# Moving the transposes inside a forward DFT from TensorE to DMA transposes

## The chip, the cores and the metric

The kernel runs on one core of a Trainium2 chip. Its time is the device time of one execution in microseconds (us); of several executions the median is taken. The core has five engines with a queue each, which run in order: PE (TensorE, matrix products), DVE (VectorE), ACT (ScalarE), POOL (GpSimd) and SP (SyncE, which here issues nearly all DMAs). The DMAs of all queues are carried by 16 DMA engines.

## The reference

The program computes one layer and all its gradients (a forward pass, then its vector-Jacobian product with `grad_out`), for one sequence of L = 2048 steps and D = 512 channels in bf16:

```
xn  = layernorm(A_u)
K   = Re( sum_n C * exp(dt*A)^l * dt*B )           # a kernel of 2048 taps per channel, N = 128 states
s   = causal_conv(xn, K)  + xn * Dskip             # the reference does it with FFTs of length 4096
g   = silu( silu(xn @ w1) @ w2 )                   # F = 1792
out = A_u + s * g
```

It returns `out` and the gradients of `A_u`, the six state matrices, `log_dt`, `Dskip`, `w1` and `w2`.

## The kernel before, in words

Time is cut as 128 partitions times T = 16 steps, channels into NB = 4 blocks of 128. The stages, in the order of the time axis of the profile (us from the start of the span):

- 0 to about 50: layer norm, tables, the parameters of the state matrices.
- 50 to about 245: `gen_ffn_fwd` (L574, both products of the FFN) beside the first part of `gen_ssm_fwd` (L509), which makes the convolution kernels `K_b` and parks the tables `XT` and `YT` of each eighth of a block in DRAM.
- 247 to about 624: `gen_conv` (L623) for blocks 0 to 3. Beside blocks 0 to 2 runs the rest of `gen_ssm_fwd`, beside block 3 the first part of `gen_ssm_bwd` (L762).
- 624 to about 710: `gen_dw2` (L661), the gradient of `w2`; 710 to about 850: `gen_dh` (L687), the gradient of the hidden layer and of `w1`; then `gen_dx` (L730) and `gen_ssm_final` (L809). `gen_ssm_bwd` runs beside these.

**One block of the convolution.** `gen_conv` makes the DFTs of the normalised input (`UX`), of the kernel `K_b` (`KX`) and, later, of the gradient (`DX`), with three products in frequency (`cplx_mul`, L135, on DVE) and three inverse DFTs (`dft_inv`, L111): the forward result `S_b`, the gradient to the input `DXC` and that to the kernel `dKs`, each written to DRAM by a DMA (L642, L645, L652, L657). The write of `dKs` (L657, to `dk_d`) is the last act of a block.

**One forward DFT** (`dft_fwd`, L78) of 2048 points for 128 channels has three steps:

1. L87: 32 small products with the table `TF` into PSUM; eight evictions by ACT (L74, 128x512 each) write them to `A` (`dftA` in the profile), real and imaginary part (c = 0, 1), reordered as 16 groups g of (t, e).
2. L95: for each of 2 x 16 blocks of 128x128 a TensorE transpose against the identity into a PSUM tile `pt_b` that holds eight; four ACT copies (L74, 128x1024 bf16) bring them to `B` (`dftB`).
3. L102 and L103: 16 products with the constant matrices C2, S2, nS2, which mix both parts of `B`; eight evictions to `X` (by ACT, or by DVE at L105 for the real part of `KX`).

`A` and `B` have one buffer each, and `dft_inv` uses the buffer of `A` as well. So a DFT cannot refill `A` before its transposes have been read, and there is no more than one DFT of a kind in flight. Four blocks of three DFTs make 12 calls.

**What sets the order.** The stages are Python generators that `interleave` (L38) merges by weights; `BoundedGen` limits how many steps of a neighbour go beside a block. That gives each instruction its place in the program. The tile framework then lays out each engine's queue itself: it takes instructions by their place in the program, but passes over one whose operands it doesn't expect yet, by its own estimate of durations. This order is fixed when the program is built; on the chip each engine follows it and waits where an operand is late. One sees it in the trace: the transposes `DOT` at L677 belong to `gen_dw2`, after block 3 in the program, and three of them are issued between 544 and 556, inside block 3.

**DMA transposes** are in the kernel already, all issued by SP with DRAM as their source: the parameters (L417), `A_ft` (L670, 128 rows of 2048, 512 KB), `DOT` (L677, 2048 rows of 128, 512 KB each), `W2T` (L673) and `W1T` (L735).

Of the kernel before, what the change touches and what calls it, by code (L numbers as in the profile page):

```python
# [11 lines left out]
BF16 = mybir.dt.bfloat16  # L12
I32 = mybir.dt.int32
AX = mybir.AxisListType
P = 128
# [62 lines left out]
def dft_fwd(k, U, X, ev, addc=None):  # L78
    nc, big, psum, psumT = k.nc, k.cbig, k.psum, k.psumT
    G = 16  # L80
    TF = k.consts["TF"]
    A = big.tile([P, 2, G, 16, 8], BF16, name="dftA", tag="dftA")
    for t0 in range(0, 16, 4):
        for c in range(2):
            ps = psum.tile([P, 4, P], F32, name="ps_s1", tag="ps")
            for j in range(4):
                nc.tensor.matmul(out=ps[:, j, :], lhsT=TF[:, t0 + j, c, :], rhs=U[:, t0 + j, :], start=True, stop=True)  # L87
            ev(A[:, c, :, t0:t0 + 4, :], ps[:].rearrange("p t (g e) -> p g t e", e=8))
        yield
    B = big.tile([P, 2, G, P], BF16, name="dftB", tag="dftB")  # L90
    for g0 in range(0, G, 8):
        for c in range(2):
            pt = psumT.tile([P, 8, P], BF16, name="pt_b", tag="pt")
            for gi in range(8):
                nc.tensor.transpose(out=pt[:, gi, :], in_=A[:, c, g0 + gi, :, :].rearrange("p t e -> p (t e)"), identity=k.ident[:])  # L95
            ev(B[:, c, g0:g0 + 8, :], pt[:])
        yield
    C2, S2, nS2 = k.consts["C2"], k.consts["S2"], k.consts["nS2"]
    for g0 in range(0, G, 4):
        for c, (m0, m1) in enumerate(((C2, S2), (nS2, C2))):  # L100
            ps = psum.tile([P, 4, P], F32, name="ps_s2", tag="ps")
            nc.tensor.matmul(out=ps[:], lhsT=m0[:], rhs=B[:, 0, g0:g0 + 4, :], start=True, stop=False)  # L102
            nc.tensor.matmul(out=ps[:], lhsT=m1[:], rhs=B[:, 1, g0:g0 + 4, :], start=False, stop=True)  # L103
            if c == 0 and addc is not None:
                nc.vector.tensor_tensor(out=X[:, c, g0:g0 + 4, :], in0=ps[:], in1=addc[:, g0:g0 + 4].unsqueeze(2).to_broadcast([P, 4, P]), op=ALU.add)  # L105
            else:
                ev(X[:, c, g0:g0 + 4, :], ps[:])
        yield
# [514 lines left out]
def gen_conv(k, b):  # L623
# [8 lines left out]
    mk = lambda nm, tag: cb.tile([P, 2, 16, P], BF16, name=nm, tag=tag)  # L632
    UX = mk("UX", "UX"); DX = mk("DX", "DX"); KX = mk("KX", "KX")
    yield from dft_fwd(k, k.xn[:, :, blk], UX, k.ev)
    yield from dft_fwd(k, k.K_b[b][:], KX, k.ev, addc=k.dskx[:, 16 * b:16 * b + 16])
    YX = mk("YX", "PX")
    cplx_mul(k, YX, KX[:], UX[:])
# [7 lines left out]
    nc.sync.dma_start(k.o0_v[:, :, blk], g_b)  # L645
    yield
    yield from dft_fwd(k, ds_b, DX, k.ev)
    cplx_mul(k, KX, KX[:], DX[:], conj_a=True)
    yield
# [264 lines left out]
```

## Time and profile before

| | |
|---|---|
| time, median of 3 (lowest to highest) | 1028.93 us (1026.76 to 1033.08) |
| profiled execution | 1033.08 us, its span 1031.3 us |
| PE, weight loads, DVE, ACT busy | 731.1, 444.3, 735.1, 619.0 us |
| queue q1 (SP's DMAs) | 147.23 MB, 54.6% of the 16 engines' span |

The profiled execution is the slowest of the three; sums below are made against it. In the page's rows of instruction groups a line reads: source line, engine, operation, written tile <- read tile, shape, count, then busy time, mean duration in ns, and idle time of the engine just before, with what ended it. L74 is the helper `Evac`, so the tile tells which eviction it is.

By convolution block, cut where `dk_d` is written, the busy time of each engine is:

| block | window | length | PE | DVE | ACT | DMA share |
|---|---|---|---|---|---|---|
| 0 | 247 to 354 | 107 | 75.6 | 103.5 | 93.6 | 0.51 |
| 1 | 354 to 468 | 114 | 81.6 | 103.5 | 99.1 | 0.39 |
| 2 | 468 to 542 | 74 | 58.0 | 42.4 | 63.4 | 0.55 |
| 3 | 542 to 624 | 82 | 62.8 | 48.2 | 68.6 | 0.76 |

### The profile page before, as it was taken

How to read it: one execution, taken by the hardware profiler on the slowest of the kernel's cores; microseconds unless marked ns; L12 is line 12 of the kernel's file. 1: busy time of each engine (PE TensorE's matmuls, PEld its weight loads, DVE VectorE, ACT ScalarE, POOL GpSimd, SP SyncE). 2: the span in 40 equal slices, each digit the busy share in tenths (PEclk: the TensorE clock that was granted, in tenths of full speed). 3: DMA queues.
4: the chain of work that ended last, by engine and by line, in shares of the span. 5: the costliest groups of instructions: out<-in, count | busy, mean ns of one | idle time of the engine just before them, and what ended most of it. 6: DMA issues, size and time to landing. Idle time of an engine off the chain costs nothing. (4 is left out here: it accounts for less than half of the span.)

```text
span 1031.3 us, 16058 instructions
## 1 busy us (share of the span) xinstructions
PE 731.1 (71%) x6215; PEld 444.3 (43%) x6281; DVE 735.1 (71%) x1196; ACT 619.0 (60%) x1062; POOL 20.7 (2%) x85
## 2 busy tenths in 40 slices
PE   0277878997866677678777774787889897699500
PEld 0144545455555465556555442333444443244200
DVE  6998888999999979996552780223756665478942
ACT  0698878898998798969879771111332434344110
POOL 2100000000000000001100000000000000000000
PEclk9878989998989888879989998899999998699855
DMA  5064655667327312642589499998544647676410
GB/s 117 10 214 168 170 194 170 210 227 183 110 63 188 81 62 62 168 89 103 106 167 208 112 203 241 203 235 201 163 153 140 177 123 199 184 219 187 114 25 22
DMA packets 240383, 154.03 MB, mean 149 GB/s; under 512 B 175729, under 2 KB 209906, under 8 KB 240306
## 3 DMA queue, kind: packets, MB, share of 16 engines
q1 hardware_dynamic: 238962, 147.23, 54.6%
q0 software_dynamic: 768, 3.67, 1.1%
q10 hardware_dynamic: 576, 2.10, 0.6%
q8 instruction: 49, 0.80, 0.3%
q14 instruction: 28, 0.23, 0.1%
HBM read 74.84 MB, written 62.13 MB: 133 GB/s over the span
## 5 line engine op out<-in xcount | busy, mean ns | idle before, releaser
L74 ACT CAST Vb<-psV 128x512 bf16<-128x512 f32 x128 | 67.5, 624 | 76.0 <-PE psV L785 75.4
L506 DVE TENSOR_TENSOR X<-T_511 128x1024 bf16<-128x1024 bf16 x128 | 84.4, 704 | 14.7 <-PE ps_k L556 14.7
L532 PE MATMUL pf_t<-ident_bfloat_78,X 128*128 128x128 bf16 x1024 | 76.6, 230 | 22.9 <-DVE X L506 8.6
L532 PEld LDWEIGHTS <-X 128*128 128x128 bf16 x1024 | 67.9, 104 | 33.3 <-issue 17.2
L74 ACT CAST XTf<-pf_t 128x512 bf16<-128x512 f32 x128 | 67.0, 636 | 3.6 <-PE pf_t L532 3.6
L604 PE MATMUL ps_o<-W_410,aT 128*128 128x512 bf16 x215 | 54.0, 398 | 3.5 <-ACT th_2187 L608 1.2
L590 PE MATMUL ps_h<-XNT,W_408 128*128 128x512 bf16 x210 | 53.1, 389 | 2.6 <-ACT th L594 1.5
L705 PE MATMUL ps_da<-DOT,W2T 128*128 128x512 bf16 x224 | 53.1, 379 | 0.0
L746 PE MATMUL ps_dx<-W1T,dhT 128*128 128x512 bf16 x216 | 52.3, 388 | 0.7 <-issue 0.5
L785 PE MATMUL psV<-XT,Gbd 128*128 128x256 bf16 x256 | 45.5, 301 | 9.8 <-DMA XT<-xt_d 7.7
L60 DVE TENSOR_TENSOR T_511<-PC 128x896 bf16<-128x896 f32 (+1 forms) x40 | 51.7, 1348 | 0.4 <-ACT PC L452 0.4
L74 ACT COPY DH<-pt_dh 128x1024 bf16<-128x1024 bf16 x28 | 27.9, 1033 | 37.0 <-PE pt_dh L712 36.9
L680 PEld LDWEIGHTS <-A_ft 128*128 128x128 bf16 x224 | 23.0, 106 | 59.6 <-DMA A_ft<-at_d 30.1
L74 ACT COPY dftB<-pt_b 128x1024 bf16<-128x1024 bf16 x48 | 46.0, 1052 | 2.0 <-PE pt_b L95 1.6
L785 PEld LDWEIGHTS <-Gbd 128*128 128x128 bf16 x256 | 34.1, 177 | 27.9 <-issue 23.1
L706 DVE SCALAR_TENSOR_TENSOR dhT<-th_ft,ps_da 128x512 bf16<-128x512 bf16 x56 | 35.6, 682 | 8.4 <-PE ps_da L705 8.2
L698 DVE TENSOR_SCALAR th_ft<-th_ft 128x2048 bf16<-128x2048 bf16 x14 | 9.7, 693 | 43.9 <-DMA th_ft<-th_d 43.9
L556 PEld LDWEIGHTS <-X 128*128 128x128 bf16 x1024 | 35.9, 100 | 6.1 <-issue 1.5
L87 PEld LDWEIGHTS <-TF 128*128 128x128 bf16 x384 | 28.1, 106 | 23.1 <-issue 21.7
L556 PE MATMUL ps_k<-YY,X 128*128 128x64 bf16 x1024 | 37.6, 195 | 0.4
L594 ACT ACTIVATE th<-ps_h 128x512 bf16<-128x512 f32 x56 | 37.8, 675 | 0.0
L593 ACT ACTIVATE aT<-ps_h 128x512 bf16<-128x512 f32 x56 | 37.4, 669 | 0.5 <-PE pf_t L532 0.3
(1581 smaller groups left out, 1881.0 us busy)
## 6 DMA issues: line engine op xcount, KB each, us to landing
xt_d<-XTf SPq DMA_DIRECT2D x32, 512.0 KB, 2.8
XT<-xt_d SPq DMA_DIRECT2D x32, 512.0 KB, 5.1
YT<-yt_d SPq DMA_DIRECT2D x64, 256.0 KB, 4.6
yt_d<-YTf SPq DMA_DIRECT2D x32, 256.0 KB, 2.4
th_d<-th SPq DMA_DIRECT2D x28, 256.0 KB, 2.2
at_d<-aT SPq DMA_DIRECT2D x4, 1792.0 KB, 6.9
a_ft<-at_d SPq DMA_DIRECT2D x14, 512.0 KB, 3.7
th_ft<-th_d SPq DMA_DIRECT2D x14, 512.0 KB, 4.2
```

The costliest lines, as they stand in the source:

```text
L60: nc.vector.tensor_tensor(out=out, in0=a, in1=b, op=ALU.mult)
L74: self.nc.scalar.copy(out=out, in_=in_)
L506: nc.vector.tensor_tensor(out=out.rearrange("p (r h l u) -> p r h l u", h=nh, l=4, u=2), in0=h, in1=l, op=ALU.mult)
L532: nc.tensor.matmul(out=pf[:, qi, m // 2, :], lhsT=X[:, m, q + qi], rhs=k.ident[:], start=(m % 2 == 0), stop=(m % 2 == 1))
L556: nc.tensor.matmul(out=ps[:, q].rearrange("p e j -> p (e j)"), lhsT=X[:, m, q], rhs=YY[:, m // 2, q // 2, 1, 64 * (q % 2):64 * (q % 2) + 6 ...
L590: nc.tensor.matmul(out=ps[:], lhsT=W1[:, dk, ft * P:(ft + 1) * P], rhs=XNT[:, dk, 4 * tcn:4 * tcn + 4, :], start=(dk == 0), stop=(dk == DK ...
L593: nc.scalar.activation(out=aT[:, ft, :], in_=pf, func=ACT.Silu)
L594: nc.scalar.activation(out=th[:, s], in_=pf, func=ACT.Tanh, scale=0.5)
L604: nc.tensor.matmul(out=pso[:], lhsT=aT[:, ft, tt * P:(tt + 1) * P], rhs=W2[:, ft, :], start=(ft == 0), stop=(ft == FT - 1))
L705: nc.tensor.matmul(out=ps[:], lhsT=k.W2T[:, dk, rows], rhs=k.DOT[:, dk, ls], start=(dk == 0), stop=(dk == DK - 1))
L746: nc.tensor.matmul(out=ps[:], lhsT=k.dhT[:, ft, t * P:(t + 1) * P], rhs=W1T[:, ft, :], start=(ft == 0), stop=(ft == FT - 1))
L785: nc.tensor.matmul(out=psV[:, qi].rearrange("p a b -> p (a b)"), lhsT=Gbd[:, :, :, :, 32 * (q_ // 2 % 2) + 4 * c + 2 * (q_ % 2) + q_ // 4] ...
```

## The change

Step 2 of the forward DFT is replaced. In place of 32 TensorE transposes and four ACT copies, two DMA transposes issued by SP, one for the real and one for the imaginary part, go straight from `A` to `B`, both in SBUF. Each moves 128 rows of 2048 elements (512 KB) and leaves `B` in the same layout as before. The two yields of the step become one, so a DFT has one step less in the merging of the generators.

```diff
@@ dft_fwd
     B = big.tile([P, 2, G, P], BF16, name="dftB", tag="dftB")
-    for g0 in range(0, G, 8):
-        for c in range(2):
-            pt = psumT.tile([P, 8, P], BF16, name="pt_b", tag="pt")
-            for gi in range(8):
-                nc.tensor.transpose(out=pt[:, gi, :], in_=A[:, c, g0 + gi, :, :].rearrange("p t e -> p (t e)"), identity=k.ident[:])
-            ev(B[:, c, g0:g0 + 8, :], pt[:])
-        yield
+    for c in range(2):
+        nc.sync.dma_start_transpose(out=B[:, c], in_=A[:, c].rearrange("p g t e -> p (g t e)"))
+    yield
     C2, S2, nS2 = k.consts["C2"], k.consts["S2"], k.consts["nS2"]
```

## The prediction, made before the result

> **What bounds the kernel now.** I read the page first (twelve DFTs: 48 copies of `dftB` on ACT), then the busy time of each engine by convolution block, then the timeline of ACT and PE in one DFT, then the waits, and last the rows of the DMA transposes that the kernel has already.
>
> From the page, the two groups that go (the second only in its TensorE line):
>
> ```profile
> L74 ACT COPY dftB<-pt_b 128x1024 bf16<-128x1024 bf16 x48 | 46.0, 1052 | 2.0 <-PE pt_b L95 1.6
> ```
>
> ACT spends 46.0 us on these copies; TensorE's transposes at L95 fill 29.9 us of its time between 247 and 624.
>
> The busy times by block (length; PE, PEld, DVE, ACT, POOL; clock, DMA share, GB/s):
>
> ```profile
> 247.00:354.00 107.00, 75.60 (x957) 60.86 (x961) 103.54 (x148) 93.64 (x167) 0.00 (x0) 0.89 0.51 117
> 354.00:468.00 114.00, 81.64 (x1005) 65.76 (x1009) 103.45 (x153) 99.13 (x173) 0.00 (x0) 0.85 0.39 98
> 468.00:542.00 74.00, 57.98 (x681) 43.23 (x682) 42.41 (x60) 63.44 (x117) 7.01 (x2) 0.93 0.55 127
> 542.00:624.00 82.00, 62.81 (x554) 40.19 (x554) 48.22 (x63) 68.64 (x127) 0.00 (x0) 0.98 0.76 178
> ```
>
> Two regimes. In blocks 0 and 1 DVE is busy 97% and 91% of the time: the work of `gen_ssm_fwd` bounds them. In blocks 2 and 3 DVE is at 57% and 59%, and ACT at 86% and 84%: here the chain of one block, step after step through single buffers, sets the length, and most of its steps end in an ACT eviction. The blocks follow each other without overlap: SP issues the last write of a block (L657) at 354.5, 468.3, 542.6 and 623.6, and the first eviction of the next block's `dftA` comes within some 1 us of it. `A_ft`, the first transfer of the next stage, waits for the end of block 3: it is issued at 625.5. So the chain's length passes on to what follows.
>
> One DFT on ACT (start, duration), block 1, `KX`:
>
> ```profile
> 383.20 0.79 ACT L74 CAST dftA<-ps_s_4843 128x512 bf16<-128x512 f32 x1
> 383.68 0.85 ACT L74 CAST KF<-ps_k 64x256 bf16<-64x256 f32 x2
> 384.55 3.76 ACT L74 COPY dftB<-pt_b 128x1024 bf16<-128x1024 bf16 x4
> ```
>
> From the end of the last `dftA` eviction (384.0) to a complete `dftB` (388.3) it takes 4.3 us. Read in the same way, the twelve steps take 4.2 to 6.1 us, the longer ones with an eviction of another tile in between; the mean of the eleven that I read is 4.9 us. That is the time the change replaces.
>
> The waits within 247 to 600 that concern it:
>
> ```profile
> DVE X L506 <- PE ps_k L556: 13.6, 7, 5.1
> PE pt_b L95 <- ACT dftB L74: 6.0, 9, 2.1
> ```
>
> The first shows what a held PE queue does: the longest of the seven, 5.1 us, falls at 368 to 373, while PE works off block 1's `UX` transposes and ACT's copies of them; the products `ps_k` of `gen_ssm_fwd` stand behind, and DVE runs out of buffers `X`.
>
> The transposes by DMA that exist (duration on SP's queue min/median/max in ns; then issue to landing in us):
>
> ```profile
> L670 SPq DMA_TRANSPOSE A_ft<-at_d x14: 1977/3214/5570, 625.5 to 696.6; - x14
> DMA to landing us min/median/max: 4.5/5.3/7.7
> ```
>
> ```profile
> L677 SPq DMA_TRANSPOSE DOT<-do_d x4: 3527/4052/11456, 544.9 to 596.9; - x4
> DMA to landing us min/median/max: 5.5/6.6/13.4
> ```
>
> `A_ft` has the size and shape of the new ones. The landing follows the end of the issue by 2.1 us at the median (5.3 less 3.2; `DOT` 6.6 less 4.05), and SP issues nothing else during the issue.
>
> **What the Trainium skill says.** "VectorE: DVE Perf Modes", section "The three transpose paths", gives 390 ns for one 128x128 block on TensorE and 1309 ns by DMA. The trace agrees on the direction only: in batches TensorE does eight in 0.61 us plus a copy of 1.05 us, a DMA 16 in 5.3 us. "DMA: Bandwidth & Descriptors", section "Latency and other measured facts", gives 261 GB/s for a DMA transpose with a non-contiguous middle dimension, an estimate of 2.0 us for 512 KB; the fastest `A_ft` held the queue 1.98 us, the median 3.2. "SBUF — State Buffer", section "Door 1: The DMA port swizzle", says that 16 neighbouring partitions reach four of 16 ports and measures 104 GB/s on them: were the source read 16 rows at a time, 512 KB would take an estimated 5.0 us. No run here has a transpose out of SBUF. "Issuing engines are not separate DMA queues" (the DMA page again) says that all DMAs share the same 16 engines; the trace agrees: `DOT`'s fourth transpose, just behind the 2 MB load of `DO_all`, held SP for 11.5 us.
>
> **The change, part by part.**
>
> *Removed.* Per DFT four copies (3.8 us of ACT), 32 transposes (2.5 us of PE) and the 4.9 us between `A` and `B`.
>
> *Added.* Per DFT two transposes one behind the other on SP: 2 x 3.2 + 2.1 = **8.5 us**, with `A_ft`'s median. Both ends: with `A_ft`'s fastest issue 2 x 2.0 + 2.5 = 6.5; with the 104 GB/s of the port figure 2 x 5.0 + 2.1 = 12.1. Both parts of `B` are needed for the first product of step 3, so there is no overlap with it. Difference to before: **+3.6** (+1.6 to +7.2). I take the middle, since the 4 KB runs of `A` and `at_d` are alike. In block 3, where the DMA engines are 76% busy with `XT`, `YT` and `DOT`, I take `DOT`'s rows: 2 x 4.05 + 2.5 = 10.6, difference to that block's 4.6 (mean of 4.2, 5.4, 4.2): +6.0.
>
> *Where it is exposed.* Blocks 0 and 1: DVE has other work, but PE's queue is in order. If step 3 stands in it too early, `pf_t`, `pt_t` and `ps_k` of `gen_ssm_fwd` wait behind it, and DVE with its two `X` buffers after them. I count half: 6 x 3.6 x 0.5 = 11. Block 2: all, 3 x 3.6 = 11. Block 3: all, 3 x 6.0 = 18.
>
> *SP's queue.* 24 more issues of 3.2 us are 77 us in a stage of 377 us where SP mostly waits (108.9 us for `XTf` alone at L534). What they delay: `xt_d`, `yt_d` and `K_b` writes have two buffers each behind them, `XT` and `YT` loads in block 3 are fetched a step ahead (cover about 10 us, one step of `gen_ssm_bwd` there). I cost this at nothing; without the cover it is up to 3 us per DFT in block 3, 9 us. The wait added to SP is for ACT's last `dftA` eviction, and for step 3 of the DFT before to have read `B`.
>
> *ACT's relief.* While the transposes fly, ACT is free for what today stands between the chain's evictions: four `Vb` (1.9 us) or four `XTf` (1.9 to 2.1). One such group moved into each gap of blocks 2 and 3 except one: 5 x 1.9 = -10. In blocks 0 and 1 DVE bounds, and I take nothing. The DMA engines carry 24 x 512 KB more, 12.6 MB or 8%; in 247 to 542 they are half idle.
>
> *Downstream.* Block 3 now ends 30 us later (11 + 11 + 18 - 10). In that time `gen_ssm_bwd` gets some two steps further, which then don't take PE in `gen_dh` (PE busy 124.5 of 140 us there), at about 3 us each: -6.
>
> Sum **+24 us**: 1033 to 1057 for the profiled execution. The median lies 4 us under it, so the forecast is **1053 us**. With the low end everywhere (12 x 1.6, half of it in blocks 0 and 1, less 10 and 6) it is -2, with the high end (12 x 7.2 less 16) +70.
>
> **The rivals.**
>
> *ACT and PE were what held the chain (faster).* ACT is busiest in blocks 2 and 3 and 88% in 0 and 1; 46 us of it go, and if the framework places other work into the whole gap, the chain pays only what the DMA lasts beyond that. It decides where a pair lands within the 4.9 us of today: then the ten groups of 1.9 us in blocks 2 and 3 leave the chain for nothing, and the 5.1 us waits for `ps_k` go: -19 and -6, about 1005. Against it: two issues at the fastest take 4.0 us and then 2.5 to land. Chance 0.15.
>
> *Absorbed (same).* `gen_ssm_fwd` and `gen_ssm_bwd` fill every gap and are missed less later; within 10 us, 1019 to 1039. For it: the low end above. Against it: blocks 2 and 3 have no DVE work left to fill. Chance 0.17.
>
> *Transposes out of SBUF are slow, or collide (much slower).* At 12 us a pair, exposed in all blocks, +60 to +85, about 1100. For it: DMA share of 1.06 at 591 to 602, just where the last `DX` needs its pair; there `DO_all` and `DOT` may go ahead of it. Chance 0.20.
>
> That the change doesn't do what it says is excluded by the layout: each run of 128 columns becomes one group of `B`.
>
> **Numbers.** Forecast case (1040 to 1085) 0.48, absorbed 0.17, faster 0.15, much slower 0.20. One per cent, 10 us, is about what a measurement of this kernel can tell from none. Range: from inside the faster case to the middle of the slow one, **1012 to 1105**, which leaves out some 0.07 below and 0.12 above. Slower by over 1% 0.68, within 0.17, faster 0.15.
>
> **What would show it.** SP rows `DMA_TRANSPOSE dftB<-dftA` x24 near 3.2 us, landing near 5.3; ACT busy down 46 us; PE waiting at L102 for the DMA of `dftB`, 12 times 2 to 6 us; the distances between the `dk_d` writes grown by 5, 6, 11 and 18 less relief; stages after 624 shifted, not longer. I would be wrong if the pair lands within 5 us, if the framework puts the wait where nothing stands behind it, or if `A`'s reading from SBUF takes 10 us or more.

## The result and the profile after

The changed kernel takes 1063.2 us (median of 4; 1061.6 to 1068.2), beside 1029.7 us for the kernel before (median of 4): a ratio of 1.033, 95% interval 1.029 to 1.038. It is slower by 33.5 us; 24 had been forecast. The profiled execution took 1061.63 us, its span is 1059.9 us (before 1031.3). From step 3 of the DFT on, a line's number is four lower than in the kernel before (L102 is now L98).

The new transposes in the view of the tile `dftB` (time of SP's issue in ns, min/median/max; PE's idle time in front of products that read `dftB`, in us and times, with what ended it; issue to landing in us):

```profile
L92 SPq DMA_TRANSPOSE dftB<-dftA x24: 1767/2477/4463, 260.0 to 627.5; - x24
  DMA dftB<-dftA: 47.9, 17
DMA to landing us min/median/max: 4.3/4.9/6.5
```

A transpose out of SBUF is no slower than `A_ft`'s out of DRAM (3.2 and 5.3 us). PE sat idle for 47.9 us until one had landed.

The busy times by block, cut again where `dk_d` is written (length; PE, PEld, DVE, ACT, POOL; clock, DMA share, GB/s):

```profile
249.00:368.00 119.00, 73.55 (x866) 56.68 (x870) 101.38 (x144) 84.70 (x156) 0.00 (x0) 0.80 0.61 131
368.00:483.60 115.60, 77.14 (x913) 59.94 (x914) 102.78 (x153) 88.28 (x161) 0.00 (x0) 0.81 0.53 124
483.60:567.10 83.50, 54.03 (x589) 37.90 (x590) 45.35 (x64) 53.13 (x105) 7.01 (x2) 0.86 0.70 146
567.10:659.00 91.90, 63.68 (x447) 36.31 (x448) 48.19 (x63) 56.91 (x113) 0.00 (x0) 0.85 0.88 194
```

Every block is longer, and ACT, 9 to 12 us lighter in each, is now at 64% and 62% in blocks 2 and 3, where it had been at 86% and 84%: the chain waits for something that isn't an engine. The last writes to `dk_d` are issued at 368.0, 483.6, 567.1 and 658.9. Against before that is 13.5 us later after block 0 (2.4 of it before the block begins; the write just ahead of it, of `dsk_o`, falls anywhere between 244.6 and 249.0 in the kernels below, with either kind of transpose), then 1.8, 9.2 and 10.8 more: 35.3 at the end of block 3. Of these, 34.8 are left when `gen_dh` begins (its first product, 743.7 beside 708.9), 32.7 when it ends, 30.1 at the first product of `gen_dx` and 28.6 at the end of the span.

The clock column differs too: 0.80, 0.81, 0.86 and 0.85 in the four blocks, where it had been 0.89, 0.85, 0.93 and 0.98. PE's products in these windows, without the transposes at L95, are busy for 268 us instead of 248, in nearly the same number (2815 and 2813). So a slower TensorE is a rival for the longer step; it is taken up behind `e_both`.

One DFT on PE, block 1, `KX`, whose last `dftA` eviction ends at 397.4:

```profile
396.70 0.56 PE L545 MATMUL pt_t<-ident_bfloat_78,YY 128*128 128x128 bf16 x7
401.42 0.59 PE L98 MATMUL ps_s_4735<-dftB,C_267 128*128 128x512 bf16 x1 [4.16 <-DMA dftB<-dftA]
...
403.08 1.06 PE L528 MATMUL pf_t<-ident_bfloat_78,X 128*128 128x128 bf16 x8
405.55 0.38 PE L99 MATMUL ps_s_4735<-dftB,S_275 128*128 128x512 bf16 x1 [1.41 <-DMA dftB<-dftA]
```

PE stands still for 4.2 us at the head of its queue until the real part has landed, does four products with it, some of the neighbour's work, and waits again for the imaginary part. From the last eviction to the product that needs both, 8.1 us. The same reading of all twelve DFTs gives 6.4 to 14.7 us, mean 8.4.

What the held queue does to the neighbour, on the page after and on the page before:

```profile
L502 DVE TENSOR_TENSOR X<-T_511 128x1024 bf16<-128x1024 bf16 x128 | 84.7, 706 | 33.8 <-PE ps_k L552 33.8
```

```profile
L506 DVE TENSOR_TENSOR X<-T_511 128x1024 bf16<-128x1024 bf16 x128 | 84.4, 704 | 14.7 <-PE ps_k L556 14.7
```

DVE is idle for 33.8 us in front of `X`, until `ps_k` frees a buffer; before (the second line) it was 14.7.

The longest of the twelve is the first, and SP's queue tells why (start, duration):

```profile
250.30 4.32 SPq L624 DMA_DIRECT2D cat_b<-cat_d  x3
254.67 2.33 SPq L626 DMA_DIRECT2D x_b<-in_A_u_dram  x1
257.05 2.86 SPq L530 DMA_DIRECT2D xt_d<-XTf  x1
260.01 6.12 SPq L92 DMA_TRANSPOSE dftB<-dftA  x2
```

`A` was complete at 253.9. The pair stood 6 us behind the issue of loads and a write. The other eleven have a mean of 7.9 us.

### The profile page after: what moved, and what is told of

Same layout as the page of the kernel before. It is cut to its first block, busy times and chain, and to the rows that moved or that the text cites. A ratio compares the mean times of both kernels' runs of the same rounds, so it can differ in the third digit from the quotient of the medians.

```text
span 1059.9 us, 15298 instructions
## 1 busy us (share of the span) xinstructions
PE 719.4 (68%) x5834; PEld 424.4 (40%) x5897; DVE 734.9 (69%) x1196; ACT 576.5 (54%) x1014; POOL 20.7 (2%) x85
## 2 busy tenths in 40 slices
DMA packets 290300, 166.57 MB, mean 157 GB/s; under 512 B 225649, under 2 KB 259826, under 8 KB 290226
## 5 line engine op out<-in xcount | busy, mean ns | idle before, releaser
L502 DVE TENSOR_TENSOR X<-T_511 128x1024 bf16<-128x1024 bf16 x128 | 84.7, 706 | 33.8 <-PE ps_k L552 33.8
L528 PEld LDWEIGHTS <-X 128*128 128x128 bf16 x1024 | 69.2, 106 | 43.2 <-issue 20.0
L781 PE MATMUL psV<-XT,Gbd 128*128 128x256 bf16 x256 | 42.8, 292 | 8.4 <-DMA XT<-xt_d 7.4
L74 ACT COPY DH<-pt_dh 128x1024 bf16<-128x1024 bf16 x28 | 27.9, 1035 | 36.2 <-PE pt_dh L708 36.1
L545 PE MATMUL pt_t<-ident_bfloat_78,YY 128*128 128x128 bf16 x256 | 27.4, 236 | 23.3 <-DVE YY L540 13.2
L552 PEld LDWEIGHTS <-X 128*128 128x128 bf16 x1024 | 38.6, 102 | 8.7 <-issue 5.1
L552 PE MATMUL ps_k<-YY,X 128*128 128x64 bf16 x1024 | 40.2, 199 | 2.2 <-ACT XTf L74 1.7
L74 ACT COPY YTf<-pt_t 128x1024 bf16<-128x1024 bf16 x32 | 33.7, 1059 | 6.6 <-issue 5.2
L600 PEld LDWEIGHTS <-aT 128*128 128x128 bf16 x224 | 22.1, 104 | 36.7 <-issue 18.9
```

The lines of the kernel that those rows point to most:

```text
L74: self.nc.scalar.copy(out=out, in_=in_)
L502: nc.vector.tensor_tensor(out=out.rearrange("p (r h l u) -> p r h l u", h=nh, l=4, u=2), in0=h, in1=l, op=ALU.mult)
L528: nc.tensor.matmul(out=pf[:, qi, m // 2, :], lhsT=X[:, m, q + qi], rhs=k.ident[:], start=(m % 2 == 0), stop=(m % 2 == 1))
L552: nc.tensor.matmul(out=ps[:, q].rearrange("p e j -> p (e j)"), lhsT=X[:, m, q], rhs=YY[:, m // 2, q // 2, 1, 64 * (q % 2):64 * (q % 2) + 6 ...
L600: nc.tensor.matmul(out=pso[:], lhsT=aT[:, ft, tt * P:(tt + 1) * P], rhs=W2[:, ft, :], start=(ft == 0), stop=(ft == FT - 1))
L781: nc.tensor.matmul(out=psV[:, qi].rearrange("p a b -> p (a b)"), lhsT=Gbd[:, :, :, :, 32 * (q_ // 2 % 2) + 4 * c + 2 * (q_ % 2) + q_ // 4] ...
```

## The experiments

Theory **L**: what costs is that the chain of a block has a longer step between `A` and `B`. Theory **H**: it is PE's queue, held at step 3 with the neighbours' products behind. Theory **C**: it is the load on SP's queue and the DMA engines. And a question left by the prediction: what was ACT's relief worth? Ratios below are against the kernel before in the same set of runs; "idle at X" is DVE's idle time in front of `X`, and the last column holds the four block ends.

| kernel | ratio, 95% interval | idle at X | ends of blocks 0 to 3 |
|---|---|---|---|
| before | | 14.7 | 354.5, 468.3, 542.6, 623.6 |
| changed | 1.033 (1.029 to 1.038) | 33.8 | 368.0, 483.6, 567.1, 658.9 |
| e_blk01 | 1.009 (1.006 to 1.011) | 30.0 | 366.4, 480.0, 553.3, 633.0 |
| e_blk23 | 1.014 (1.008 to 1.019) | 16.2 | 354.7, 468.1, 549.6, 639.6 |
| e_both | 1.029 (1.023 to 1.035) | 26.8 | 365.8, 480.3, 566.9, 657.2 |
| e_free | 0.971 (0.966 to 0.977) | 9.0 | 352.9, 459.8, 521.9, 595.1 |
| e_late | 1.019 (1.013 to 1.024) | 17.4 | 362.8, 470.6, 556.1, 648.3 |
| e_late_pe | 0.989 (0.986 to 0.992) | 7.0 | 351.0, 460.8, 537.2, 616.7 |
| e_load | 1.015 (1.010 to 1.021) | 20.9 | 357.8, 471.2, 551.7, 636.6 |
| f_load | 1.005 (1.003 to 1.007) | 13.5 | 355.1, 466.3, 544.2, 626.8 |
| e_pipe_dma | 0.988 (0.982 to 0.994) | 10.7 | 355.3, 461.7, 531.7, 611.4 |
| e_pipe_pe | 1.009 (1.006 to 1.011) | 10.2 | 355.7, 469.4, 549.2, 631.5 |
| f_pipe_dma | 0.983 (0.980 to 0.986) | 3.9 | 353.2, 457.8, 526.8, 606.8 |
| f_pipe_pe | 1.019 (1.014 to 1.023) | 20.7 | 361.1, 479.2, 558.2, 642.1 |

**The change in half of the blocks.**

```diff
+    if k.blk < 2:          # e_blk23: k.blk >= 2
         for c in range(2):
             nc.sync.dma_start_transpose(out=B[:, c], in_=A[:, c].rearrange("p g t e -> p (g t e)"))
         yield
+    else:
+        ...                # step 2 of the kernel before, two yields
```

> DMA transposes in the DFTs of blocks 0 and 1 only; blocks 2 and 3 as before. Theory L (the loss is the longer step between A and B in the chain of a block, whole in blocks 2 and 3, half in 0 and 1): the block ends of the changed kernel moved by 13.5 and then 1.8 us in blocks 0 and 1, so about 12 to 15 us over the kernel before, 1042 to 1045. Theory H (PE held at step 3 starves gen_ssm_fwd and so DVE, which happens beside blocks 0 to 2): most of the loss, 20 to 30 us, 1050 to 1060.

> DMA transposes in blocks 2 and 3 only. Theory L: the block ends moved by 9.2 and 10.8 us there, less some 6 that come back after block 3: 12 to 16 us over before, 1042 to 1046. Theory H: 5 to 10 us, 1035 to 1040. If the two halves add up to less than the 33 us of the whole, the rest is interplay, such as gen_ssm_fwd ending later.

Measured: 1040.6 and 1045.7 us, beside 1031.5 for the kernel before. The rows of the two pages for `X`, `e_blk01` first:

```profile
L511 DVE TENSOR_TENSOR X<-T 128x1024 bf16<-128x1024 bf16 x128 | 83.6, 693 | 30.0 <-PE ps_k L561 30.0
```

```profile
L511 DVE TENSOR_TENSOR X<-T 128x1024 bf16<-128x1024 bf16 x128 | 84.3, 701 | 16.2 <-PE ps_k L561 16.2
```

DVE's stall of 30 us comes with blocks 0 and 1, as H has it, but costs only 9 us in the end (6 to 12): block 0 ends 11.9 us late and nothing is added after. Blocks 2 and 3, almost without that stall, cost 14 us (7.0 and 8.9 by their ends). That is L's division, a little under it in the first half, and not H's. The two together are 23 us; some 10 us of the whole are interplay, or lie in the intervals; the runs don't tell which.

**ACT's relief taken back.** Transposes and copies are done as before, but into a spare tile.

```diff
+    S = big.tile([P, 8, P], BF16, name="dftS", tag="dftS")
     for c in range(2):
         nc.sync.dma_start_transpose(out=B[:, c], in_=A[:, c].rearrange("p g t e -> p (g t e)"))
-    yield
+    ...                    # the loop of the kernel before, with its two yields
+            ev(S[:], pt[:])
```

> The DMA transposes make B as in the changed kernel, and the 32 TensorE transposes and four ACT copies are done as well, into a spare tile that nothing reads. So the relief of ACT (46 us) and PE is taken back and the DMA stays. If the relief was worth the 10 us that the prediction gave it, or more, the time rises from 1063 to 1073 or above; if ACT has slack all through, it stays within 4 us of 1063.

Measured: 1062.4 us, as the changed kernel, with ACT busy for 622.9 us instead of 576.5. By the expectation ACT has slack all through. One reserve: this kernel has the two yields of the kernel before, the changed one has one, and the runs on yields below show that a yield is worth several us. So the relief is worth something between nothing and those few us; the 10 us of the prediction it isn't.

The clock in the four blocks is 0.86, 0.87, 0.84 and 0.91 in this kernel, higher than in the changed one except in block 2, and the time is the same; the overlapped kernel below is ahead of the kernel before at 0.85, 0.87, 0.90 and 0.89. This speaks against the clock as the main cause. What part of the loss goes with it was not separated.

**No step 2 at all.** Step 3 reads `A` as it is.

```diff
-    B = big.tile([P, 2, G, P], BF16, name="dftB", tag="dftB")
-    for c in range(2):
-        nc.sync.dma_start_transpose(out=B[:, c], in_=A[:, c].rearrange("p g t e -> p (g t e)"))
+    B = A[:].rearrange("p c g t e -> p c g (t e)")
```

> Step 2 is left out: step 3 reads A in the place of B, untransposed, so neither TensorE, ACT nor DMA work stands between steps 1 and 3. This is the floor of any way to do the transposes. Theory L: the step of 4.9 us goes from the chain, 6 x 4.9 x 0.5 in blocks 0 and 1 and 6 x 4.9 in blocks 2 and 3, less 10 that come back later: 35 us under before, about 995. If DVE alone bounded blocks 0 to 3, within 15 us of before, 1015 to 1030.

Measured: 1000.5 us, 31 under the kernel before. So the step by TensorE and ACT costs 31 us and by DMA, in the same place of the order, some 64. The second figure compares two kernels with one yield each; the first doesn't, since the kernel before has two, so it is rather too low (the runs on yields below). Blocks 2 and 3 are 12.2 and 7.9 us shorter than before, block 1 is 6.9 and block 0 only 1.6: in the main L's picture again, for the way back.

**The step later in the program, and its control.** Two more yields after step 2, in the changed kernel (`e_late`) and in the kernel before (`e_late_pe`).

```diff
         nc.sync.dma_start_transpose(out=B[:, c], in_=A[:, c].rearrange("p g t e -> p (g t e)"))
     yield
+    yield
+    yield
```

> The changed kernel with two more yields between the transposes and step 3, so that one more step of the neighbouring generator stands ahead of step 3 in the program. Theory H (neighbours caught behind step 3 in PE's queue are what is lost): 8 to 15 us under the changed kernel, 1048 to 1055. Theory L (the chain itself is longer): no better than 1058, since the chain's own order is unchanged.

> The control to e_late: the kernel before with the same two yields between the copies to B and step 3. If the 14 us that e_late won are due to the wait for the landing being further back in PE's queue, this is within 6 us of before or slower; if they are only the other merging of the generators, it is 10 us or more under before, 1010 to 1020.

Measured: 1049.1 us, 14 under the changed kernel, as H had it; but the control gains 12 us as well (1014.5 beside 1026.1). The waits of `e_late` (engine, line, what it waited for: us in total, times, longest):

```profile
PEld L100 <- DMA dftB<-dftA: 45.6, 12, 9.0
PE ps_s L100 <- DMA dftB<-dftA: 37.4, 11, 8.9
...
DVE X L504 <- PE ps_k L554: 16.3, 3, 10.9
```

PE still waits for the landing in all twelve DFTs. In the changed kernel the first of these lines reads:

```profile
PEld L98 <- DMA dftB<-dftA: 51.5, 12, 9.1
```

PE's idle time in front of products of `dftB` falls from 47.9 to 39.9 us, so most of the wait is where it was. DVE's idle time at `X` is halved in both forms, from 33.8 to 17.4 us and from 14.7 to 7.0. So most of the gain is the other merging of the generators, which helps either form, and H's reason for it falls in the main; the 4 us by which the DMA form gains more lie within the intervals. It leaves a point that the prediction had overlooked: the change itself takes one yield out of each DFT. From one yield to three the DMA form gains 1.45% (1.033 to 1.019), from two to four the other form 1.1%, so one yield is worth an estimated 6 to 7 us; at an equal count the DMA transposes cost an estimated 25 to 27 us and the lost yield the rest. No run has plain DMA and TensorE forms with the same number of yields, so this division is interpolated, not shown.

**The load alone.** The step of the kernel before makes the result, in place in `X`, and the DMA pair goes out of `A` into the buffer that this frees, and nobody reads it.

```diff
-    B = big.tile([P, 2, G, P], BF16, name="dftB", tag="dftB")
+    B = X
+    S = big.tile([P, 2, G, P], BF16, name="dftS", tag="dftS")
+    for c in range(2):
+        nc.sync.dma_start_transpose(out=S[:, c], in_=A[:, c].rearrange("p g t e -> p (g t e)"))
     ...                    # step 2 of the kernel before
```

> The transposes of the kernel before (TensorE and ACT, now written into X, which step 3 then overwrites group by group, so that dftB's buffer is free) and, beside them, the two DMA transposes out of A into that free buffer, which nothing reads. The load on SP, the DMA engines and the hold on A is that of the changed kernel, but no product waits for it. Theory L (only the wait for the landing costs): within 6 us of before, 1025 to 1037. Theory C (SP's queue and the DMA engines are what costs): 15 to 33 us over before.

`e_load` measured 1044.0 us and tells nothing of C: in it the product for the imaginary part of a group reads the group's real part after its eviction, so it isn't the DFT and waits once more in every group. The same holds for `e_pipe_dma` and `e_pipe_pe` below. With both products ahead of both evictions:

> As e_load, with both products of a group of step 3 ahead of both evictions, so that the DFT is computed in place without the extra wait. Theory L and H (what costs is that products wait for the landing): within 6 us of before, 1023 to 1036. Theory C (SP's queue, the DMA engines, the hold on A): 12 us or more over before.

Measured: 1032.0 us beside 1026.1, +5 us (3 to 7). All 24 transposes are in it, with landings of 4.9 us as in the changed kernel. Taken as it stands, the load on SP, the DMA engines and the hold on `A` is worth some 5 us, not 33: C falls as the main cause, and a small cost stays with it. One reserve: the transposes in place and the new order of the products are in this kernel too, and what they do alone was not measured.

**The landing covered.** The three DFTs of a block overlap in the program, `A` has two buffers, and the transposes write `X` in place of `B`, so the second buffer needs no more space than before. In the last two of these four kernels both products of a group stand ahead of both evictions, as in `f_load`.

```diff
-    yield from dft_fwd(k, k.xn[:, :, blk], UX, k.ev)
-    yield from dft_fwd(k, k.K_b[b][:], KX, k.ev, addc=k.dskx[:, 16 * b:16 * b + 16])
+    yield from dft_fwd(k, k.xn[:, :, blk], UX, k.ev)      # steps 1 and 2 alone
+    yield from dft_fwd(k, k.K_b[b][:], KX, k.ev)
+    yield from dft_out(k, UX, k.ev)                       # step 3
+    yield from dft_fwd(k, ds_b, DX, k.ev)
+    yield from dft_out(k, KX, k.ev, addc=k.dskx[:, 16 * b:16 * b + 16])
     ...
-    yield from dft_fwd(k, ds_b, DX, k.ev)
+    yield from dft_out(k, DX, k.ev)
```

> The changed kernel with A in two buffers, the transposes written into X in place of B, and the DFTs of a block overlapped in the program: step 1 of UX, step 1 of KX, step 3 of UX, step 1 of DX, step 3 of KX, and step 3 of DX where its DFT stood. A pair then flies under the next DFT's step 1. Theory L: nearly all of the loss goes and part of the step of 4.9 us as well, 1005 to 1030. If the loss is SP's queue or the DMA engines (theory C), 1050 to 1065.

> The same overlap with the transposes of the kernel before. Theory L: the chain gains here too, but by less, since TensorE and ACT do the step themselves; 1010 to 1028. If it is under the overlapped DMA form by 5 us or more, DMA transposes are no gain even where they are covered; if over it, relief of ACT counts once the chain is short.

> As e_pipe_dma, with the same mend: the three DFTs of a block overlapped, A in two buffers, transposes by DMA into X. e_pipe_dma had 1016.7 with a wait too many in each group; without it 1000 to 1014. Theory L and H: under the kernel before by 15 us or more. Theory C: not under 1020.

> As e_pipe_pe, with the same mend: the overlap with transposes by TensorE and ACT. If the gain of the overlapped DMA form is the overlap and the second buffer alone, this is as fast, within 5 us. If, once covered, DMA transposes also relieve ACT, this is slower than f_pipe_dma by 8 to 20 us.

Measured for the last pair, the whole DFT in both: **1008.2 us** with DMA transposes, 0.983 of the kernel before (0.980 to 0.986) and so ahead of both kernels; 1047.9 us with TensorE and ACT. The transposes of `UX` in the fast one, their waits in all, and the row of `X` on its page:

```profile
L92 SPq DMA_TRANSPOSE UX<-dftA x8: 1793/2658/4685, 260.2 to 534.8; - x8
  DMA UX<-dftA: 2.0, 2
...
DMA to landing us min/median/max: 4.3/5.7/6.8
```

```profile
L511 DVE TENSOR_TENSOR X<-T 128x1024 bf16<-128x1024 bf16 x128 | 83.4, 691 | 3.9 <-PE ps_k L561 3.8
```

The transposes land about as late as in the changed kernel or later (5.7 us here, 4.8 for `KX` and 5.3 for `DX`, beside 4.9), and PE waits for them 2.0 us in place of 47.9; for `KX` and `DX` not at all. The loss is gone, and with it more than half of what the step itself costs: by the ratios (0.983 and 0.971) some 12 us are left over the kernel without step 2. L and H both forecast this, so it speaks against C and doesn't divide the two; that was done by the halves of the blocks. The other form doesn't gain by the overlap but loses 1.9%; it is 40 us behind the overlapped DMA form, where at most 8 to 20 us had been expected. In it DVE waits 26.1 us in five waits for step 3 of `KX` (14.1 us in the fast one), and 20.7 us at `X`; why this order suits it so badly stays open. `e_pipe_pe`, with its wait too many, had lost only 0.9%, so the order of the products alone moves this form by some 10 us. The 40 us between the two forms are therefore not all relief of ACT and PE.

## The prediction against the runs, step by step

- **Direction and main cause: right.** The pair replaces a shorter step in the chain of a block, and hiding its landing takes the loss away.
- **The longer step: +3.6 us forecast, +3.7 measured** from the last eviction of `dftA` to the last eviction of `X` (mean of twelve: 10.2 us before, 14.0 after). The first DFT has +9.3, by SP's queue, the other eleven +3.2. There is luck in the agreement: the 4.9 us of the prediction run to the complete `dftB`, but the kernel before starts step 3 when half of it is there (in the DFT that the prediction shows, L103 at 387.0, `dftB` complete at 388.3), and the changed one starts it with the real part. Neither overlap was in the sum, and they balance.
- **The pair: 8.5 us forecast, 8.4 measured** (mean from the last eviction to the first product with both parts), but made up otherwise: the issue takes 2.5 us at the median, not 3.2, the landing comes 2.4 us after it, and the rest is for the most part time in SP's queue. Without the first DFT the mean is 7.9. In block 3, 7.6, 8.3 and 10.5 us were measured where 10.6 was put: `DOT`'s rows were too slow a model.
- **"Both parts of `B` are needed for the first product": wrong.** L98 reads the real part alone and starts at the first landing, four times in the DFT shown. The evictions still wait for the second.
- **SP's queue "at nothing": too low.** The first pair lost 6 us there, and `f_load` puts the whole load at 5 us. The 6 us are part of the term that was mis-sized, block 0: 5.5 us forecast, 11 measured (13.5 less the 2.4 of its later start).
- **The lost yield: not costed at all.** It was described, but no price put on it; the runs with more yields make it worth an estimated 6 to 7 us.
- **Exposure by block:** forecast 5.5, 5.5, 7 and 12 net of relief; measured 11, 1.8, 9.2 and 10.8. The sum was good (30 forecast; 33 measured, 35 with the later start). The three DFTs of a block grew by 15.2, 6.7, 10.8 and 12.2 us from `dftA` to `X`, so blocks 0 and 1 together show 59% of it and blocks 2 and 3 87%, where half and all had been assumed. The division between blocks 0 and 1 was not foreseen. In block 1, where little shows, DVE is busy for 102.8 of 115.6 us.
- **ACT's relief, -10: not found.** With the copies back in place the time stays. Block 3 came near its net figure because its steps grew by 12.2 us, not 18; block 2 came out over it.
- **Downstream, -6: the number came, the reason didn't.** 35.3 us at the end of block 3 are 28.6 at the end of the span, -6.7. But `gen_ssm_bwd` gets no step further: its products `psV` fall 64, 16, 56 and 120 on block 3 and the three stages after it in both kernels. Of the 6.7 us, 2.6 come between the last write of `dhT` in `gen_dh` (850.4; 883.1) and the first product of `gen_dx`, where PE does 135 products in both, in 24.9 us instead of 27.9, at a clock of 0.90 instead of 0.79. Nor does a later block 3 explain it: from the end of block 3 to the end of the span there are 407.7 us before and 401.0 after, but also only 404.4 in `e_free`, whose block 3 ends 28.5 us early. This term was right by luck, and what causes the gain stays open.
- **From span to median:** the sum reached 1057 us where the profiled execution took 1061.6. That the median lies 4 us under the profiled execution held for the kernel before alone, whose profiled execution was its slowest, and did not carry over. That is half of the 10 us by which the forecast was low.
- **The faster rival** needed a pair within 4.9 us or gaps well filled. In this order neither came; in `f_pipe_dma` other work fills the time of the landing, with the same transposes. The much slower rival, pairs of 12 us, came once in twelve, by SP's queue.

## What to carry to other kernels

A transfer that takes the place of engine work trades busy time for latency. In the chain through single buffers here the latency was what counted, though ACT's share of busy time fell from 86% to 64% in block 2. Before such an exchange, look for a step without dependence on it that can run meanwhile, and give the source a second buffer: here the same transposes went from 33 us lost to 17 us won by the order and the buffers around them. The same order with TensorE's transposes lost 1.9%, so measure it with the form you mean to use. And count what an edit does to the order: a yield fewer is a change too, and a control with the old form tells its share.

## What was not expected of the hardware

In the changed kernel a DMA transpose of 128 rows of 2048 elements out of SBUF held SP's queue for 1.8 us at the least and 2.5 at the median, and landed after 4.9; out of DRAM, in the same shape, it was 3.2 and 5.3 (`A_ft`, on DMA engines that were 93% busy). The estimate of 5.0 us from four SBUF ports, after the Trainium skill's "SBUF — State Buffer", section "Door 1: The DMA port swizzle", does not hold for it: from issue to landing, all included, it took 4.3 us at the least and 4.9 at the median. Each transpose adds some 2080 packets of under 512 bytes to the profile's count (225649 less 175729, by 24).
